# Re-timing the side work of a software-pipelined FNet and gated-convolution kernel

## The chip, the core and the metric

The kernel runs on one core of a Trainium2 chip. The metric is the device time of one execution in microseconds (us), as the median of repeated runs. The engines are named as in the profile: PE (TensorE matmuls), PEld (its weight loads), DVE (VectorE), ACT (ScalarE), POOL (GpSimd), SP (SyncE, which only issues transfers here).

## What is computed

```python
x: (8, 3136, 256) float32
X = np.fft.fft(np.fft.fft(x, axis=1), axis=2).real       # FNet mixing
h = np.maximum(X @ w_in, 0.0)                            # (8, 3136, 1024)
hp = h padded by one row of zeros at both ends of the sequence
conv_out = sum(conv_w[k] * hp[:, k:k + 3136] for k in range(3))
out = (h / (1 + np.exp(-conv_out))) @ w_out              # (8, 3136, 256)
```

All of it is float32. There are eight batches; the sequence transform of a batch has 3136 points.

## The kernel before

**Main pipeline.** The sequence is cut by symmetry into four chunks of output rows per batch (`CUTS`), and the 1024 hidden features into `NF` = 8 blocks of 128. A step is one (batch, chunk, feature block): 8 x 4 x 8 = 256 steps, 32 to a batch (`per`). The loop at the end of the kernel runs over cycles t, and one cycle holds stages of several steps. This is the order in which a cycle hands its instructions to the in-order queues of the engines:

- `sigmoid(t-2)` on ACT (L713)
- `products(t+1)`: the matmuls of `pb` and `pa` on PE, which finish the transforms and apply the input weights (tiles `qt`, `pt`, `G`); `copies(t+1)` on ACT brings `pb` to SBUF (L677)
- the side work "act"
- `combine(t)` on DVE: adds `pa` and the copy and clips at zero (two instructions, L688), which gives `h`
- the side work "load", then the side work "dve"
- `seed(t+2)` and `first_tap(t)` on ACT (L643, L694)
- `other_taps(t-1)` on DVE (two instructions, L700)
- `gate(t-2)`: one half of the product with the sigmoid on POOL (L720), the other on DVE (L721; L723 for a rest in the last chunk)
- `mm2(t-3)` on PE: twelve matmul instructions into `po`, fourteen in the last chunk of every second batch; after the eighth feature block ACT copies the result out and SP stores it
- the side work "pe"

PSUM has one buffer for `pb`, two for `pa`, four for `po` and one (`pd`) for the side work.

**Side work.** While the steps of batch b-1 run, batch b is prepared by operations that the table `side` spreads over the cycles, through `at(cycle, where, fn)`:

- *Loads* (`load_ops`): half a batch is one plain load and, for the second half, three one-row loads, all from SP, and four indirect loads (`mirrored`, L133), which POOL issues.
- *Folds* (`fold_ops`): 14 operations per batch on DVE, seven per half (`pair`, `both`, `evens`, `feats`; L158 to L187), which add and subtract mirrored rows and columns.
- *Sums of the DFT* (`units`): eight units per batch, each of four products on PE (`Unit.matmuls`, into `pd`), where needed a copy on ACT (`Unit.copy`, L287 and L306), and two sums on DVE (`Unit.fin`, L291/L294, L310/L312, L322/L324). Two units of a batch have no copy. A unit's copy and sums stand in the cycle after its last product, and in that cycle DVE runs the sums between `combine` and `other_taps`.
- *The column* (`Feature`): one column of the transform that needs a small DFT of its own. `place` loads tables, `gather` fetches 3136 single elements per batch into `ft`, `tables` and `stage` compute. It is done twice, for batches 1 to 3 and 4 to 7.

In the kernel before, the folds of batch b occupy the cycles from the end of the previous folds to `stop`, evenly spread, and the products of batch b run from `stop` to cycle 32b-3:

```python
    for b in range(1, B):
        stop = per * (b - 1) + max(28 - 8 * b, 2)
        fold_at[b] = (end, stop - end)
        dft_at[b] = (stop, per * b - 3 - stop)
        end = stop
```

So `stop` is 20, 44, 68, 98, 130, 162 and 194. Folds of batch b+1 and units of batch b lie over the same cycles, with no regard for each other. The loads of the next batch start in the cycle after the last fold of the half they replace, two indirect loads to a cycle. The gathers of the column go out from ACT, three in cycle 7 and four in cycle 20.

Of the kernel before, what the change touches and what calls it, by code (L numbers as in the profile page):

```python
# [31 lines left out]
RC = 56  # L32
# [6 lines left out]
def kernel(  # L39
# [10 lines left out]
    nc = tc.nc  # L50
    B, S, D = x.shape
    F = moe_w_in.shape[1]
    P = 128
# [9 lines left out]
    NF = F // P  # L63
# [27 lines left out]
    act = nc.scalar.activation  # L91
# [19 lines left out]
    def load_ops(b, h, eng, other=None, held=False):  # L111


        def plain():
            t = xp.tile([P, 8, 2, D], F32, name="xh", tag="xh")
            xh[b, h] = t
            if held:

                nc.gpsimd.memset(t[0:1, 0, 0, 0:1], 0.0)
            eng.dma_start(out=t[0:NP, 0:4], in_=bass.AP(  # L120
                tensor=x.tensor, offset=x.offset + (b * S + 1 + 2 * h) * D,
                ap=[[HQ * D, NP], [Q4 * D, 4], [1, 2 * D]]))

        def zero():
            t = xh[b, h]
            for s0, n, r in ((0, 4, 0), (4, 3, 1), (7, 1, 0)):
                (other or eng).dma_start(out=t[NP:KR, s0:s0 + n], in_=bass.AP(
                    tensor=x.tensor, offset=x.offset + (b * S + r * Q4) * D,
                    ap=[[D, 1], [Q4 * D, n], [0, 2], [1, D]]))

        def mirrored(m):
            def f():
                nc.gpsimd.indirect_dma_start(  # L133
                    out=xh[b, h][0:NP, 7 - m].rearrange("p q d -> p (q d)"),
                    out_offset=None,
                    in_=bass.AP(tensor=x.tensor, offset=x.offset,
                                ap=[[2 * D, B * S // 2], [1, 2 * D]]),
                    in_offset=bass.IndirectOffsetOnAxis(ap=idx[0:NP, 0:1], axis=0),
                    element_offset=(b * S + (4 - m) * Q4 - HO + 2 * (1 - h)) * D)
            return f  # L140
        return [plain] + [zero] * h + [mirrored(m) for m in range(4)]

    def fold_ops(b):

        def half(h):
            k = slice(0, NP if h == 0 else KR)
            qs = slice(2 * h, 2 * h + 2)  # L150

            def t():
                return xh[b, h]

            def pair(m):
                def f():
                    a, r = t()[k, m:m + 2], t()[k, 7 - m:5 - m:-1, ::-1, :]
                    vt(a[:, :, :, 1:D], a[:, :, :, 1:D], r[:, :, :, D - 1:0:-1], op=ALU.add)  # L158
                    if m == 2:
                        a, r = t()[k, 0:4], t()[k, 7:3:-1, ::-1, :]  # L160
                        vt(a[:, :, :, 0], a[:, :, :, 0], r[:, :, :, 0], op=ALU.add)
                return f

            def flat(i, j):
                return t()[k, i:j].rearrange("p s q d -> p (s q d)")

            def both(to, op):
                def f():
                    vt(flat(to, to + 2), flat(0, 2), flat(2, 4), op=op)  # L169
                return f  # L170

            def evens():
                vt(flat(0, 1), flat(4, 5), flat(5, 6), op=ALU.add)
                vt(flat(1, 2), flat(4, 5), flat(5, 6), op=ALU.subtract)  # L174

            def feats(odd):
                def f():
                    if h == 0 and odd:
                        wt[b] = [wp.tile([P, 4, HQ, P], F32, name="w", tag="w%d" % i) for i in range(2)]
                        if b == 0:  # L180
                            ea[b] = ep.tile([P, 2, HQ], F32, name="ea", tag="ea")
                            nc.gpsimd.memset(wt[b][0][0:KR, 2:4, :, P - 1:P], 0.0)
                    w, s = wt[b][odd], 6 * odd
                    v = t()[k, s:s + 2]
                    lo, hi = v[:, :, :, 1:P], v[:, :, :, D - 1:P:-1]
                    vt(w[k, 0:2, qs, 1:P], lo, hi, op=ALU.add)  # L186
                    vt(w[k, 2:4, qs, 0:P - 1], lo, hi, op=ALU.subtract)  # L187
                    nc.gpsimd.tensor_copy(w[k, 0:2, qs, 0], v[:, :, :, 0])  # L188
                    if b:
                        nc.gpsimd.memset(wt[b][odd][k, 2:4, qs, P - 1:P], 0.0)  # L190
                    elif odd:
                        gt(w[k, 2:4, qs, P - 1], t()[k, 7:5:-1, :, P], sg[k], op=ALU.mult)
                    else:
                        nc.gpsimd.tensor_copy(ea[b][k, :, qs], v[:, :, :, P])
                return f

            return [pair(0), pair(2), both(6, ALU.subtract), feats(1), both(4, ALU.add), evens,
                    feats(0)]

        return half(0) + half(1)  # L200
# [173 lines left out]
    class Feature:  # L374
# [39 lines left out]
                        tensor=dft_seq.tensor, offset=dft_seq.offset + (2 * r + s) * NQ * HE,  # L414
                        ap=[[4 * NQ * HE, n], [HE, NQ], [1, w]]))

        def gather(self, b0, b1):
            for b in range(b0, b1):
                nc.scalar.dma_start(out=self.y[self.K, b - b0].unsqueeze(2), in_=bass.AP(  # L419
                    tensor=x.tensor, offset=x.offset + b * S * D + P,  # L420
                    ap=[[RC * D, RC], [D, RC], [1, 1]]))

        def tables(self, i):
            H, K = self.H, self.K
# [40 lines left out]
    def spread(b, cs):  # L465

        for c in cs:
            ch = chunks[c]
            eb[b, c] = ebp.tile([P, HN], F32, name="eb", tag="eb")[:, 0:ch.k1 - ch.k0]
            nc.sync.dma_start(out=eb[b, c], in_=ed[b:b + 1, ch.k0:ch.k1].to_broadcast([P, ch.k1 - ch.k0]))  # L470
# [284 lines left out]
    begin, us, row, flip, store = units(0)  # L755
# [37 lines left out]
    per = len(chunks) * NF  # L793
    side = {}

    def at(cycle, where, fn):
        side.setdefault((cycle, where), []).append(fn)
# [9 lines left out]
        at(NF + 1 + j // 3, "load", fn)  # L807


    fold_at, dft_at = {}, {}  # L810
    end = 9
    for b in range(1, B):
        stop = per * (b - 1) + max(28 - 8 * b, 2)
        fold_at[b] = (end, stop - end)
        dft_at[b] = (stop, per * b - 3 - stop)
        end = stop
    for b in range(1, B):
        ops = fold_ops(b)
        c0, n = fold_at[b]
        cs = [c0 + j * n // len(ops) for j in range(len(ops))]  # L820
        assert b > 1 or cs[7] > NF + 3
        if b + 1 < B:
            for h in range(2):
                c1 = cs[7 * h + 6] + 1
                for j, fn in enumerate(load_ops(b + 1, h, nc.sync)):
                    at(c1 + (j + 1) // 2, "load", fn)
        for j, fn in enumerate(ops):
            at(cs[j], "dve", fn)
        begin, us, *_ = units(b)
        us = us[0:4] + us[5:]  # L830
        c0, n = dft_at[b]
        at(c0, "pe", begin)
        cs = [c0 + i * n // len(us) for i in range(len(us) + 1)]
        for i, u in enumerate(us):
            k = cs[i + 1] - cs[i]
            for j in range(k):
                at(cs[i] + j, "pe", lambda u=u, j=j, k=k: u.matmuls(j, k))
            at(cs[i + 1], "act", u.copy)
            at(cs[i + 1], "dve", u.fin)
        at(cs[-1] - 2, "load", lambda b=b: spread(b, range(len(chunks) - 1)))  # L840
        at(per * b + 1, "load", lambda b=b: spread(b, [len(chunks) - 1]))

    feat = Feature()
    at(5, "load", feat.place)
    for c, b0, b1 in ((7, 1, min(4, B)), (20, 4, B)):
        at(c, "load", lambda b0=b0, b1=b1: feat.gather(b0, b1))
    for i in range(3):
        at(11 + i, "act", lambda i=i: feat.tables(i))
    for c, b0, b1 in ((14, 1, min(4, B)), (per, 4, B)):
        for i, where in enumerate(("pe", "dve", "pe", "act")):  # L850
            at(c + i + (i > 2), where, lambda i=i, b0=b0, b1=b1: feat.stage(i, b0, b1))

# [1 line left out]
    n = len(steps)  # L856
# [4 lines left out]
    for t in range(n + LAG):  # L861
        def run(where):
            for fn in side.get((t, where), []):
                fn()
        if 0 <= t - 2 < n:
            sigmoid(steps[t - 2])
        if t + 1 < n:
            products(steps[t + 1])
            copies(steps[t + 1])
        run("act")  # L870
        if t < n:
            combine(steps[t])
        run("load")
        run("dve")
        if t + 2 < n:
            seed(steps[t + 2])
        if t < n:
            first_tap(steps[t])
        if 0 <= t - 1 < n:
            other_taps(steps[t - 1])  # L880
        if 0 <= t - 2 < n:
            gate(steps[t - 2])
        if t >= LAG:
            mm2(steps[t - LAG])
        run("pe")
# [66 lines left out]
```

## Time and profile before

| | |
|---|---|
| time, median of 3 runs | 1238.14 us (1236.81 to 1238.31) |
| profiled span | 1236.5 us |
| PE, DVE, ACT, POOL busy | 1189.9, 1136.0, 878.1, 378.4 us |
| matmuls of `mm2` (`po`) | 3072 instructions, 711.6 us |
| taps on DVE (L700) | 512 instructions, 555.5 us |
| chain that ended last | PE 71%, DVE 18%, issue 4%, ACT 3% |

In the timeline each line has the start, the busy time, the engine, the line of the kernel, the operation with its output and inputs, how many equal instructions were merged, and in brackets the engine's idle time before it with what ended it. A busy PE is a model of pipelined matmuls, so the length of a cycle is best read from the start of one `pb<-qt,G` group to the start of the next. In the table of windows each engine's column is its busy time in that stretch with the number of instructions.

### The profile page before, as it was taken

To read this page: it belongs to the slowest core of one execution; us is meant where nothing else is said; L and a number is where in the kernel's file an instruction comes from. 1 tells how busy PE (TensorE), PEld (TensorE's weight loads), DVE (VectorE), ACT (ScalarE), POOL (GpSimd) and SP (SyncE) were. 2 spreads that over 40 slices of the span, in tenths; PEclk is the share of its full clock that TensorE was granted. 3 is DMA by queue.
4 is the path that set the end of the run, shared out by engine and by line. 5 is a ranking of instruction groups with operands and counts; after the bars stand their busy time and mean duration, and the time that the engine had idled before them with its cause. 6 is when DMAs were issued, how large, how long until landed. Compare 5 with 4: busy or idle time off the path is not lost.

```text
span 1236.5 us, 15434 instructions
## 1 busy us (share of the span) xinstructions
PE 1189.9 (96%) x4876; PEld 908.4 (73%) x4876; DVE 1136.0 (92%) x1696; ACT 878.1 (71%) x1832; POOL 378.4 (31%) x474
## 2 busy tenths in 40 slices
PE   5998989899999999999999999999999999999998
PEld 4666667677777777677777777777777777777776
DVE  7799979999999989999999999999899888899996
ACT  2467646686677776777777777787777777788884
POOL 5225431433324241342324223242122211222222
PEclk9999999999999999999999999999999999999999
DMA  9504241211222120210212111120001000110000
GB/s 226 183 7 79 79 55 46 85 28 52 65 66 76 33 65 14 75 56 26 79 38 67 31 52 52 45 86 26 9 18 52 31 26 27 39 39 27 26 27 30
DMA packets 70213, 66.30 MB, mean 54 GB/s; under 512 B 28123, under 2 KB 57827, under 8 KB 70131
## 3 DMA queue, kind: packets, MB, share of 16 engines
q1 hardware_dynamic: 42443, 52.09, 13.7%
q0 software_dynamic: 5120, 12.85, 3.5%
q10 hardware_dynamic: 22568, 0.36, 1.3%
q8 instruction: 39, 0.64, 0.2%
q14 instruction: 43, 0.35, 0.1%
HBM read 39.53 MB, written 25.74 MB: 53 GB/s over the span
## 4 chain that ended last, share of the span: by engine, by line
PE 71%; DVE 18%; issue 4%; ACT 3%; DMA 1%; ACTq 0%; SPq 0%; DVEq 0%
PE po L94 43%; PE pb L94 10%; PE pa L94 10%; PE pd L94 7%; DVE g L700 6%; DVE g L721 2%; DVE h L688 2%; DVE xh L158 2%; ACT nb L677 1%; DVE w L187 1%; DVE xh L169 1%; DVE w L186 1%; DMA xh<-in_x_dram 1%; ACT g L713 1%; ACTq L419 0%
## 5 line engine op out<-in xcount | busy, mean ns | idle before, releaser
L94 PE MATMUL po<-wout,g 128*128 128x256 f32 x3072 | 711.6, 381 | 18.2 <-DVE g L721 18.2
L94 PEld LDWEIGHTS po<-wout,g 128*128 128x128 f32 x3072 | 580.8, 190 | 173.0 <-DVE g L721 50.0
L700 DVE SCALAR_TENSOR_TENSOR g<-h,cw,g 128x770 f32<-128x770 f32 (+1 forms) x512 | 555.5, 1085 | 9.8 <-ACT g L694 0.7
L720 POOL TENSOR_TENSOR g<-g,h 128x385 f32<-128x385 f32 (+1 forms) x256 | 241.0, 942 | 793.3 <-ACT g L713 536.3
L713 ACT ACTIVATE g<-g 128x385 f32<-128x385 f32 (+2 forms) x512 | 244.4, 527 | 200.7 <-DVE g L700 199.5
L677 ACT ACTIVATE nb<-pb 128x386 f32<-128x386 f32 (+2 forms) x472 | 208.2, 494 | 81.4 <-PE pb L94 80.5
L688 DVE CUSTOM_DVE_ANT_0 h<-pa,nb 128x386 f32<-128x386 f32 (+2 forms) x492 | 255.5, 559 | 3.7 <-ACT h L674 3.7
L694 ACT ACTIVATE g<-h,cw 128x770 f32<-128x770 f32 (+1 forms) x256 | 243.6, 951 | 0.2 <-DVE h L688 0.2
L94 PE MATMUL pa<-pt,G 128*128 128x387 f32 (+2 forms) x512 | 212.5, 496 | 7.5 <-ACT pa L643 7.5
L94 PE MATMUL pb<-qt,G 127*128 127x387 f32 (+2 forms) x512 | 212.6, 496 | 0.0
L643 ACT ACTIVATE pa<-eb,ge 128x387 f32<-128x387 f32 (+2 forms) x252 | 151.8, 603 | 15.8 <-issue 11.6
L94 PEld LDWEIGHTS pa<-pt,G 128*128 128x128 f32 x512 | 96.6, 189 | 82.1 <-issue 18.6
L721 DVE TENSOR_TENSOR g<-g,h 128x385 f32<-128x385 f32 (+1 forms) x256 | 145.4, 568 | 1.4 <-ACT g L713 1.4
L94 PE MATMUL pd<-tab,w 98*128 98x196 f32 (+3 forms) x448 | 120.9, 374 | 0.0
L94 PEld LDWEIGHTS pb<-qt,G 127*128 127x128 f32 x512 | 94.7, 190 | 17.4 <-issue 1.0
L133 POOL DMA_INDIRECT xh<-in_x_dram,idx x64 | 97.9, 1529 | 15.4 <-issue 13.0
L94 PEld LDWEIGHTS pd<-tab,w 98*128 98x128 f32 (+1 forms) x448 | 83.6, 190 | 12.7
L740 ACT COPY os<-po 128x256 f32<-128x256 f32 x196 | 58.2, 394 | 8.5 <-PE po L94 5.5
L158 DVE TENSOR_TENSOR xh<-xh 98x1020 f32<-98x1020 f32 (+1 forms) x32 | 46.7, 1465 | 3.8 <-DMA xh<-in_x_dram,idx 3.8
L169 DVE TENSOR_TENSOR xh<-xh 98x1024 f32<-98x1024 f32 (+1 forms) x32 | 40.6, 1269 | 0.1
L188 POOL COPY w<-xh 98x4 f32<-98x4 f32 (+1 forms) x32 | 27.4, 856 | 13.3 <-DVE xh L174 7.4
L291 DVE TENSOR_TENSOR qt<-as,pd 128x197 f32<-128x197 f32 (+1 forms) x14 | 7.2, 514 | 19.9 <-ACT as L287 19.9
(114 smaller groups left out, 392.8 us busy)
## 6 DMA issues: line engine op xcount, KB each, us to landing
out_dram<-os SPq DMA_DIRECT2D x192, 128.0 KB
xh<-in_x_dram SPq DMA_DIRECT2D x16, 784.0 KB
eb<-ed SPq DMA_DIRECT2D x16, 193.5 KB
tab<-dft_seq_dram SPq DMA_DIRECT2D x4, 589.5 KB
raw<-in_moe_w_in_dram SPq DMA_DIRECT2D x4, 512.0 KB
raw<-in_moe_w_out_dram SPq DMA_DIRECT2D x1, 2048.0 KB
eb<-ed SPq DMA_DIRECT2D x8, 209.0 KB
eb<-ed SPq DMA_DIRECT2D x8, 193.0 KB
```

The costliest lines, as they stand in the source:

```text
L94: nc.tensor.matmul(o, l, r, start=start, stop=stop, skip_group_check=True)
L133: nc.gpsimd.indirect_dma_start(out=xh[b, h][0:NP, 7 - m].rearrange("p q d -> p (q d)"), out_offset=None, in_=bass.AP(tensor=x.tensor, offs ...
L158: vt(a[:, :, :, 1:D], a[:, :, :, 1:D], r[:, :, :, D - 1:0:-1], op=ALU.add)
L643: act(pa[s][:, 0:n], eb[b, c], AF.Copy, scale=ge[:, f:f + 1])
L677: act(nb[s][:, i, cols], p[:, cols], AF.Copy, scale=-1.0 if i else 1.0)
L688: nc.vector._custom_dve(TENSOR_ADD_SAT, out=to, in0=a[:, cols], in1=c[:, i, cols], s0=BIG, s1=0.0)
L694: act(gs[s], hs[s][:, 0:n], AF.Copy, scale=cw[:, 0, s[2]:s[2] + 1])
L700: stt(out=g, in0=h[:, k:k + n], scalar=cw[:, k, f:f + 1], in1=g, op0=ALU.mult, op1=ALU.add)
L713: act(gs[s][:, c], gs[s][:, c], AF.Sigmoid)
L720: gt(g[:, p], g[:, p], h[:, p], op=ALU.mult)
L721: vt(g[:, v], g[:, v], h[:, v], op=ALU.mult)
L740: nc.scalar.copy(out=osb[:, j % 2], in_=pt[:, j % 2])
```

## The change

The change re-times the side work; it neither adds nor removes a computation.

- Folds get cycles of their own. The set `taken` collects the cycles that hold a unit's sums or the DVE stage of the column, and `free` moves a fold to the next cycle that is not taken, one fold to a cycle. This holds for batches 2 to 7; batch 1 keeps its cycles.
- The boundaries `ends` replace `stop`: 20, 46, 72, 98, 125, 157, 189. From batch 5 on the products of a batch take 32 cycles, one product to a cycle.
- The side work "load" is emitted after `gate`, where it stood before the side work "dve". Indirect loads go one to a cycle.
- The gathers of the column go out from SP, one to a cycle: cycles 6 to 8 and 21 to 24. The second run of the column's stages starts a cycle earlier (31).

```diff
-        def gather(self, b0, b1):
-            for b in range(b0, b1):
-                nc.scalar.dma_start(out=self.y[self.K, b - b0].unsqueeze(2), in_=bass.AP(
-                    tensor=x.tensor, offset=x.offset + b * S * D + P,
-                    ap=[[RC * D, RC], [D, RC], [1, 1]]))
+        def gather(self, b, b0):
+            nc.sync.dma_start(out=self.y[self.K, b - b0].unsqueeze(2), in_=bass.AP(
+                tensor=x.tensor, offset=x.offset + b * S * D + P, ap=[[RC * D, RC], [D, RC], [1, 1]]))
...
+    ends = [9] + [max(26 * b - 6, per * (b - 1) - 3) for b in range(1, B)]
+    taken = set()
+    def free(cycle):
+        while cycle in taken:
+            cycle += 1
+        taken.add(cycle)
+        return cycle
...
+    for c, b0, b1 in ((6, 1, min(4, B)), (21, 4, B)):
+        for b in range(b0, b1):
+            at(c + b - b0, "load", lambda b=b, b0=b0: feat.gather(b, b0))
-    for c, b0, b1 in ((14, 1, min(4, B)), (per, 4, B)):
+    for c, b0, b1 in ((14, 1, min(4, B)), (per - 1, 4, B)):
...
+        taken.add(c + 1)
...
             at(cs[i + 1], "dve", u.fin)
+            taken.add(cs[i + 1])
...
-        cs = [c0 + j * n // len(ops) for j in range(len(ops))]
+        cs = [free(c0 + j * n // len(ops)) if b > 1 else c0 + j * n // len(ops) for j in range(len(ops))]
...
-                c1 = cs[7 * h + 6] + 1
                 for j, fn in enumerate(load_ops(b + 1, h, nc.sync)):
-                    at(c1 + (j + 1) // 2, "load", fn)
+                    at(cs[7 * h + 6] + 1 + j, "load", fn)
...
             combine(steps[t])
-        run("load")
         run("dve")
...
             gate(steps[t - 2])
+        run("load")
         if t >= LAG:
             mm2(steps[t - LAG])
```

More of the change, by code (lines that the diff above doesn't have):

```diff
@@ L807 @@
         at(NF + 1 + j // 3, "load", fn)
-    fold_at, dft_at = {}, {}
-    end = 9
-    for b in range(1, B):
[L813 to L819, printed above, removed]
-        cs = [c0 + j * n // len(ops) for j in range(len(ops))]
-        assert b > 1 or cs[7] > NF + 3
-        if b + 1 < B:
-            for h in range(2):
-                c1 = cs[7 * h + 6] + 1
-                for j, fn in enumerate(load_ops(b + 1, h, nc.sync)):
-                    at(c1 + (j + 1) // 2, "load", fn)
-        for j, fn in enumerate(ops):
-            at(cs[j], "dve", fn)
+    ends = [9] + [max(26 * b - 6, per * (b - 1) - 3) for b in range(1, B)]
[5 more added lines that the diff above has]
+        return cycle
+    feat = Feature()
+    at(5, "load", feat.place)
+    for c, b0, b1 in ((6, 1, min(4, B)), (21, 4, B)):
+        for b in range(b0, b1):
+            at(c + b - b0, "load", lambda b=b, b0=b0: feat.gather(b, b0))
+    for i in range(3):
+        at(11 + i, "act", lambda i=i: feat.tables(i))
+    for c, b0, b1 in ((14, 1, min(4, B)), (per - 1, 4, B)):
+        for i, where in enumerate(("pe", "dve", "pe", "act")):
+            at(c + i + (i > 2), where, lambda i=i, b0=b0, b1=b1: feat.stage(i, b0, b1))
+        taken.add(c + 1)
+    for b in range(1, B):
         begin, us, *_ = units(b)
         us = us[0:4] + us[5:]
-        c0, n = dft_at[b]
-        at(c0, "pe", begin)
+        c0, n = ends[b], per * b - 3 - ends[b]
+        at(max(c0, per * (b - 1) + 1), "pe", begin)
         cs = [c0 + i * n // len(us) for i in range(len(us) + 1)]
@@ L839 @@
             at(cs[i + 1], "dve", u.fin)
+            taken.add(cs[i + 1])
         at(cs[-1] - 2, "load", lambda b=b: spread(b, range(len(chunks) - 1)))
         at(per * b + 1, "load", lambda b=b: spread(b, [len(chunks) - 1]))
[L843 to L848, printed above, removed]
-    for c, b0, b1 in ((14, 1, min(4, B)), (per, 4, B)):
-        for i, where in enumerate(("pe", "dve", "pe", "act")):
-            at(c + i + (i > 2), where, lambda i=i, b0=b0, b1=b1: feat.stage(i, b0, b1))
+    for b in range(1, B):
+        ops = fold_ops(b)
+        c0, n = ends[b - 1], ends[b] - ends[b - 1]
+        cs = [free(c0 + j * n // len(ops)) if b > 1 else c0 + j * n // len(ops) for j in range(len(ops))]
+        assert cs[-1] < ends[b] and (b > 1 or cs[7] > NF + 3)
+        if b + 1 < B:
+            for h in range(2):
+                for j, fn in enumerate(load_ops(b + 1, h, nc.sync)):
+                    at(cs[7 * h + 6] + 1 + j, "load", fn)
+        for j, fn in enumerate(ops):
+            at(cs[j], "dve", fn)
     LAG = 3
```

## The prediction

> **What bounds the kernel now.** I read the table of windows first, because a share of busy time over the whole span mixes stages. I cut it at starts of the `pb<-qt,G` matmuls, that is at cycles of the loop: rows 1 to 4 below are cycles 66-97, 98-129, 130-161 and 162-193 (32 each), row 5 is cycles 194-221 (the sums of batch 7, no folds), row 6 is 24 cycles near the end with no side work at all.
>
> ```profile
> core 0: us, PE busy (x) PEld busy (x) DVE busy (x) ACT busy (x) POOL busy (x), PEclk, DMA share, GB/s
> 384.54:529.90 145.36, 141.66 (x580) 107.97 (x579) 137.36 (x209) 107.25 (x223) 49.25 (x58) 1.00 0.19 58
> 529.90:675.21 145.31, 143.42 (x591) 110.62 (x590) 136.61 (x210) 108.43 (x224) 47.59 (x57) 1.00 0.16 51
> 675.21:818.99 143.78, 140.90 (x580) 108.35 (x579) 135.82 (x205) 106.96 (x222) 46.38 (x56) 1.00 0.16 51
> 818.99:964.30 145.31, 143.41 (x592) 110.61 (x591) 136.01 (x210) 108.45 (x224) 38.45 (x51) 1.00 0.10 32
> 964.30:1088.11 123.81, 123.81 (x516) 96.66 (x515) 104.21 (x158) 94.27 (x198) 25.32 (x33) 1.00 0.10 33
> 1092.28:1185.75 93.47, 93.47 (x386) 72.82 (x385) 92.62 (x129) 78.73 (x164) 23.27 (x33) 1.00 0.08 26
> ```
>
> Rows 5 and 6 have no gap on PE: there PE is the bound. Row 6 gives a bare cycle: 93.47 / 24 = 3.895 us. The timeline adds: 0.105 for a last-chunk `products`, 0.43 where `mm2` has fourteen matmuls, about 0.34 for a product of 196 columns and 0.66 for one of 392. Row 5 checks it: 123.81 less 28 x 3.895, 8 x 0.105 and 0.43 leaves 13.5 us for a batch's 32 products. So PE alone would need 124.64 + 0.84 + 13.5 = 139.0 us for a batch, plus 0.43 for each long `mm2` (1, 7, 1, 7 in rows 1 to 4): 139.5, 142.1, 139.5, 142.1. Measured less this floor: 5.8, 3.2, 4.2, 3.2. The same sum gives 3.1 for cycles 46-65 and 7.9 for cycles 22-45. That is 27.4 us in which PE waits, and folds are present in all of it.
>
> Then the table of waits, for who ends them:
>
> ```profile
> PEld po L94 <- DVE g L721: 50.0, 68, 2.9
> ```
>
> `mm2` waits for DVE's half of the gate. The timeline of cycle 143, where a fold (L186, L187) shares the cycle with a unit's sums (L291, L294), shows how:
>
> ```profile
> 735.29 0.52 DVE L291 TENSOR_TENSOR qt<-as,pd 128x196 f32<-128x196 f32 x1 [1.06 <-ACT as L287]
> 735.65 0.52 DVE L294 TENSOR_TENSOR qt<-pd,as 128x196 f32<-128x196 f32 x1
> 736.00 0.68 DVE L186 TENSOR_TENSOR w<-xh 98x508 f32<-98x508 f32 x1
> 736.60 0.67 DVE L187 TENSOR_TENSOR w<-xh 98x508 f32<-98x508 f32 x1
> 737.20 2.07 DVE L700 SCALAR_TENSOR_TENSOR g<-h,cw,g 128x770 f32<-128x770 f32 x2
> 739.18 0.56 DVE L721 TENSOR_TENSOR g<-g,h 128x385 f32<-128x385 f32 x1
> 739.65 0.56 DVE L688 CUSTOM_DVE_ANT_0 h<-pa,nb 128x386 f32<-128x386 f32 x1
> ```
>
> ```profile
> 739.79 0.48 PE L94 MATMUL po<-wout,g 128*128 128x256 f32 x1 [0.78 <-DVE g L721]
> ```
>
> The sums wait for ACT's copy, which uses up whatever DVE was ahead; then the fold delays taps and gate by 737.20 - 736.00 = 1.20 us, and PE waits. The cycle takes 5.27 instead of 4.23.
>
> Last, the gathers in cycle 20, in ACT's timeline and in PE's, and the clock after them:
>
> ```profile
> 160.10 4.58 ACTq L419 DMA_DIRECT2D ft<-in_x_dram  x2
> 164.74 0.59 ACT L643 ACTIVATE pa<-eb,ge 128x387 f32<-128x387 f32 x1 [6.78 <-issue]
> ```
>
> ```profile
> 165.38 1.36 PE L94 MATMUL pa<-pt,G 128*128 128x387 f32 x2 [3.78 <-ACT pa L643]
> ```
>
> ```profile
> 165.72:169.12 3.40, 3.40 (x9) 2.37 (x8) 1.12 (x3) 3.40 (x8) 1.94 (x3) 0.50 0.46 3
> ```
>
> ACT is held by issuing, so its `seed` is late, PE stands 3.78 us, and its clock is then halved for 3.4 us. Cycle 21 takes 12.27 us against a floor of 6.54: 5.7 lost.
>
> [...] here gaps of 3.78 and 2.28 us sufficed while one of 2.83 us at 92.86 did not. [...] a POOL gate behind two indirect loads at 744.03 meets the taps, which take 2.77 instead of 2.07 us.
>
> **The change part by part.**
>
> *Folds.* I keep an account of DVE's slack, from trace numbers alone. DVE's own cycle is 3.39 us (from L700 at 737.20 to the next at 740.59), 0.35 more in the last chunk. So a cycle gains slack of its floor less 3.39: 0.5 bare, 0.85 with a short product, 1.2 with a long one. A fold costs 1.2; sums cost 0.55, 0.7 or 1.0 by kind; the column's DVE stage costs 1.1. Sums that wait for a copy set the slack to about 0.1 in a cycle of 4.23 (in cycle 143 the fold cost 1.20 and PE lost 1.04), to more in longer ones. Slack holds at most 4 us: `gate(t-3)` may run almost two cycles late. What goes below zero PE waits.
>
> Run over the old order it gives, for cycles 22-45, 46-65 and the four rows above: 4.7, 3.7, 5.8, 3.4, 4.6, 3.4, against 7.9, 3.1, 5.8, 3.2, 4.2, 3.2 read. It falls short only in 22-45, where PE's clock was halved once (1.7) and the column's stages stand. Run over the new order: 8.6, 1.9, 3.9, 2.1, 3.3, 1.7. For instance before, cycle 143 lost 1.1 and cycle 157 (sums and `evens` together) 1.7; after, the sums of 141 leave 0.08, the folds of 142 and 143 cost 0.35 each beyond the 0.85 regained, and 0.24 and 0.47 are lost. From cycle 46 on that is 20.9 before and 12.9 after in the account; scaled to the 19.5 read, 12.0 remain: **7.5 us won**.
>
> Cycles 22-45 go the other way. Before, folds stood free of charge beside sums in cycles 23, 25, 26, where four products make PE's floor 5.3 to 6.5 us. Now `taken` pushes them past 29, and cycles 30, 31, 33 to 40 hold a fold each and 32 the column's stage, with bare PE cycles of 3.9. Each loses 1.2 - 0.5 = 0.7: 8.6 in all, against 7.9 read before with its halved clock. **0.7 lost.** No gap there exceeds 1.3 us, so I expect no halving.
>
> *Gathers.* ACT's seven issues, 0.85 to 2.9 us each, go to SP. What is queued behind them on SP: in cycles 6 to 8 the plain load of cycle 9, which waits for `w_out` to be narrowed in cycle 7 anyway; in 21 to 24 three one-row loads and, from cycle 26, stores. The first users are the matmuls of cycles 14 and 31. The first group waits on PE for matmuls that have long run, the second for the column's earlier stages. Nobody on the path waits for SP then. So the 5.7 of cycle 21 come back whole. In cycle 8 (7.65 us, its like take 4.54) only about half of 3.1 does: DVE narrows weights until 93.02, its gate starts at 95.01, and `mm2` waits for that instead. **7.2 won.**
>
> *Loads behind the gate, one a cycle.* POOL idles most of the time; nothing waits for L720 in the table of waits. What goes is the collision above: the 60 taps in such cycles took 3.4 us over the normal, nearly all within the slack. **0.3 won**, 0 to 2. The later loads have five cycles or more before their fold, against 3.9 us to land (transfer list). In the instruction order `place` now has DVE wait for POOL behind its gate in cycle 5, up to 1 us; but `seed` no longer stands behind its four issues on ACT (2.85 us of wait before). I take zero for both.
>
> Sum: 7.5 - 0.7 + 7.2 + 0.3 = 14.3; 1238.1 - 14.3 = 1223.8, rounded to **1224 us**.
>
> **Rivals.**
>
> *Folds give little.* DVE is busy 136 us of 144 a batch either way. If folds back to back after sums lose what was won, or a fold after sums costs 1 us rather than 0.3, the fold part shrinks to zero: 1238 - 7 = 1231. For it: pairs 126/127, 142/143, 158/159 stand together. Against: the account fits the old order to 0.6 us per stretch.
>
> *More is won.* Staggered loads also remove collisions on the slack, and cycle 8 comes back whole: 4 us more, 1220, or 1216 with the folds' loss halved again. For: L700 ranges to 2.77. Against: these slow taps are few.
>
> *Slower.* The packed folds of cycles 28 to 44 cost 1.3 each because DVE meets POOL's gate (up to 0.5 a cycle), [...] and SP's issues delay stores or the `eb` rows for batch 1: 15 lost against 13 won, about 1240. Against: SP mostly waits for ACT's copies (850 us of waits).
>
> **How the numbers follow.** Forecast (1219 to 1228) 0.60; little from folds (1228 to 1234) 0.22; more won (1214 to 1219) 0.09; no change 0.04; slower 0.05. Faster is the sum of the first three, 0.91. The range for 8 in 10 is 1217 to 1232.
>
> **What would show it.** Right: in the windows of cycles 98-193 about 1.5 us less per 32; no cycle over 10 us in the first 250 us, and PEclk at 1.00 there; no wait of ACT L643 on issue; seven gathers on SP's queue. Wrong: PE waits for L721 after cycle 98 as often as before, or a new wait for SP's transfers (`eb`, `xh`) on ACT or DVE.

## The result and the profile after

The changed kernel takes 1223.7 us (median of 4 runs, 1223.19 to 1223.94) against 1238.2 for the kernel before, timed beside it. The ratio is 0.9885, with a 95% interval of 0.9867 to 0.9902. The profiled span is 1222.2 instead of 1236.5 us.

I cut the trace again at the starts of the `pb<-qt,G` matmuls, which in the changed kernel fall at 375.44, 520.46 and so on for the same cycles 66, 98, 130, 162 and 194. This is the table of windows of the kernel after, with the columns as before:

```profile
core 0: us, PE busy (x) PEld busy (x) DVE busy (x) ACT busy (x) POOL busy (x), PEclk, DMA share, GB/s
375.44:520.46 145.02, 142.03 (x579) 108.11 (x578) 138.00 (x211) 107.25 (x223) 44.10 (x58) 1.00 0.18 57
520.46:666.66 146.20, 145.66 (x601) 112.28 (x600) 138.26 (x214) 107.97 (x224) 53.21 (x60) 1.00 0.17 55
666.66:808.54 141.88, 140.96 (x579) 108.52 (x578) 133.99 (x206) 107.46 (x223) 45.20 (x56) 1.00 0.17 52
808.54:951.92 143.38, 143.07 (x591) 110.97 (x590) 131.98 (x206) 108.23 (x223) 30.28 (x48) 1.00 0.09 28
```

The second row is longer than before (146.20 against 145.31), and that is no loss: it now holds batch 5's first products (601 matmuls instead of 591), which stood in the third row. PE's idle part, sum less busy, shows the gain: 1.9, 2.9 and 1.9 us in rows 2 to 4 before, 0.5, 0.9 and 0.3 now. In the first row it stays: 3.7 before, 3.0 now.

Here are cycles 141 to 143 of the kernel after, DVE's timeline:

```profile
716.91 0.52 DVE L291 TENSOR_TENSOR qt<-as,pd 128x196 f32<-128x196 f32 x1 [1.58 <-ACT as L287]
717.27 0.52 DVE L294 TENSOR_TENSOR qt<-pd,as 128x196 f32<-128x196 f32 x1
717.62 2.04 DVE L698 SCALAR_TENSOR_TENSOR g<-h,cw,g 128x770 f32<-128x770 f32 x2
719.58 0.56 DVE L719 TENSOR_TENSOR g<-g,h 128x385 f32<-128x385 f32 x1
720.05 1.02 DVE L686 CUSTOM_DVE_ANT_0 h<-pa,nb 128x386 f32<-128x386 f32 x2
720.99 1.27 DVE L158 TENSOR_TENSOR xh<-xh 99x1020 f32<-99x1020 f32 x1
722.18 2.06 DVE L698 SCALAR_TENSOR_TENSOR g<-h,cw,g 128x770 f32<-128x770 f32 x2
724.16 0.55 DVE L719 TENSOR_TENSOR g<-g,h 128x385 f32<-128x385 f32 x1
```

The sums still wait for ACT's copy (1.58), but the taps follow them at once. The fold (L158) comes a cycle later, when some slack has been regained. PE feels a fold one cycle after DVE runs it, because `mm2` takes the gate of the cycle before: the 5.27 us that the prediction gives for cycle 143 are, counted at the `pb<-qt,G` starts, those of cycle 144 (cycle 143 itself took 4.23). In the changed kernel cycle 142, after the sums, takes 4.23 us, its floor. Cycle 143, after the first fold, takes 4.41, and cycle 144, after the second, 4.71: 0.17 and 0.48 over their floors. Before, the one fold behind the sums cost 1.04.

The gathers of batches 4 to 7 in SP's timeline, and ACT's copy and seed in cycle 21, both after:

```profile
151.98 0.91 SPq L418 DMA_DIRECT2D ft<-in_x_dram  x1
152.93 5.65 SPq L127 DMA_DIRECT2D xh<-in_x_dram  x3
158.69 4.92 SPq L418 DMA_DIRECT2D ft<-in_x_dram  x3
```

```profile
159.67 0.32 ACT L306 COPY as<-pd 128x196 f32<-128x196 f32 x1
159.87 0.61 ACT L641 ACTIVATE pa<-eb,ge 128x387 f32<-128x387 f32 x1
```

SP is busy issuing from 151.98 to 163.61 and nobody waits for it; the seed follows the copy without a gap. SP waits for nobody either, so the gathers of cycles 22 to 24 leave back to back, all before cycle 22 begins on PE (164.50): "one to a cycle" is the order in the program, not in time. Cycle 21 takes 6.53 us instead of 12.27.

In the chain that ended last, DVE has a larger share than before (18%) and PE a smaller one (71%). It is one chain of many, and I rest nothing on it:

```profile
PE 68%; DVE 22%; issue 4%; ACT 2%; DMA 0%; DVEq 0%; SPq 0%; ACTq 0%
```

### The profile page after: what moved, and what is told of

Read it like the earlier page. It is cut to its first block, busy times and chain, and to the rows that moved or that the text cites. A ratio compares the mean times of both kernels' runs of the same rounds, so it can differ in the third digit from the quotient of the medians.

```text
span 1222.2 us, 15450 instructions
## 1 busy us (share of the span) xinstructions
PE 1187.9 (97%) x4876; PEld 907.5 (74%) x4876; DVE 1126.0 (92%) x1696; ACT 877.0 (72%) x1832; POOL 370.9 (30%) x474
## 4 chain that ended last, share of the span: by engine, by line
PE 68%; DVE 22%; issue 4%; ACT 2%; DMA 0%; DVEq 0%; SPq 0%; ACTq 0%
PE po L94 42%; PE pb L94 10%; PE pa L94 10%; DVE g L698 7%; PE pd L94 7%; DVE h L686 4%; DVE g L719 3%; DVE xh L158 2%; DVE xh L169 1%; ACT nb L675 1%; DVE w L186 1%; DVE w L187 1%; DVE xh L173 0%; ACT g L711 0%; DVE pt L291 0%
## 5 line engine op out<-in xcount | busy, mean ns | idle before, releaser
L94 PE MATMUL po<-wout,g 128*128 128x256 f32 x3072 | 709.9, 381 | 13.8 <-DVE g L719 13.3
L698 DVE SCALAR_TENSOR_TENSOR g<-h,cw,g 128x770 f32<-128x770 f32 (+1 forms) x512 | 548.9, 1072 | 9.3 <-ACT g L692 0.2
L718 POOL TENSOR_TENSOR g<-g,h 128x385 f32<-128x385 f32 (+1 forms) x256 | 232.5, 909 | 781.3 <-ACT g L711 523.1
L133 POOL DMA_INDIRECT xh<-in_x_dram,idx x64 | 106.5, 1665 | 13.4 <-issue 9.6
L94 PEld LDWEIGHTS pd<-tab,w 98*128 98x128 f32 (+1 forms) x448 | 84.0, 191 | 12.5
L158 DVE TENSOR_TENSOR xh<-xh 98x1020 f32<-98x1020 f32 (+1 forms) x32 | 40.8, 1283 | 2.4 <-DMA xh<-in_x_dram,idx 2.4
L291 DVE TENSOR_TENSOR pt<-as,pd 128x197 f32<-128x197 f32 (+1 forms) x14 | 7.3, 520 | 20.2 <-ACT as L287 20.2
```

Source lines behind the costliest of these rows:

```text
L94: nc.tensor.matmul(o, l, r, start=start, stop=stop, skip_group_check=True)
L133: nc.gpsimd.indirect_dma_start(out=xh[b, h][0:NP, 7 - m].rearrange("p q d -> p (q d)"), out_offset=None, in_=bass.AP(tensor=x.tensor, offs ...
L698: stt(out=g, in0=h[:, k:k + n], scalar=cw[:, k, f:f + 1], in1=g, op0=ALU.mult, op1=ALU.add)
L718: gt(g[:, p], g[:, p], h[:, p], op=ALU.mult)
```

## The experiments

Each kernel was traced and timed beside the kernel before. To compare them, I took the length of every cycle from the timeline and subtracted the floor of the prediction. The sum over a stretch is the time that PE lost there, in us:

| kernel | time, us | ratio to before (95%) | cycles 0-21 | 22-45 | 46-193 |
|---|---|---|---|---|---|
| before | 1238.0 to 1238.6 | | 22.1 | 7.9 | 19.5 |
| after | 1223.7 | 0.9885 (0.9867-0.9902) | 13.8 | 9.1 | 12.5 |
| e1 gathers only | 1231.4 | 0.9945 (0.9929-0.9962) | 16.2 | 7.2 | 19.6 |
| e2 loads only | 1231.8 | 0.9947 (0.9930-0.9964) | 18.6 | 6.7 | 19.0 |
| e3 folds only | 1233.3 | 0.9958 (0.9944-0.9972) | 23.3 | 10.1 | 13.5 |
| e4 gathers from ACT | 1223.4 | 0.9881 (0.9864-0.9897) | 13.9 | 9.1 | 12.2 |
| e5 before, folds ahead | 1227.6 | 0.9904 (0.9887-0.9920) | 24.6 | 7.9 | 7.0 |
| e6 e5 with e1 and e2 | 1214.1 | 0.9802 (0.9786-0.9818) | 14.4 | 6.0 | 5.8 |
| e7 batch 2 shares | 1219.7 | 0.9849 (0.9832-0.9865) | 13.9 | 5.8 | 12.2 |
| e8 loads ahead | 1223.7 | 0.9881 (0.9864-0.9897) | 15.0 | 9.1 | 12.2 |
| e9 after, folds ahead | 1211.4 | 0.9781 (0.9767-0.9794) | 14.4 | 3.9 | 5.6 |
| e10 e9, other `ends` | 1210.9 | 0.9770 (0.9757-0.9783) | 15.2 | 3.9 | 4.2 |

The start of the loop, which no edit touches, moves by up to 2 us from trace to trace (42.5 to 44.6 us). So the stretches tell more than the totals. A constant in the floor of a stretch falls out when two kernels are compared; only such differences are used below.

**e1: the gathers alone.** The kernel before with the changed `gather`:

```diff
-        at(c, "load", lambda b0=b0, b1=b1: feat.gather(b0, b1))
+        for b in range(b0, b1):
+            at(c + b - b0, "load", lambda b=b, b0=b0: feat.gather(b, b0))
```

> The kernel before, with only the gathers changed (from SP, one a cycle, cycles 6-8 and 21-24). Theory (ACT held by issuing costs PE the wait, and the halved clock after it): cycle 21 falls from 12.3 to 6.5-7 us, cycle 8 from 7.65 to about 6.3, PEclk 1.00 until cycle 33, everything after cycle 22 as before; 8 us less, about 1230. Rival (the gathers only move their cost, to SP's stores and eb rows, and the fold schedule carries the gain): 2 us less or nothing.

Cycle 21 fell to 6.53 and cycle 8 to 6.27, and cycles 46-193 did not move: the theory holds. But 5.9 us were won in cycles 0-21, less than expected. Cycles 8 to 13 take 31.42 us against 31.57 before: what cycle 8 won (1.38), cycles 10 to 13 gave back. PE's wait in cycle 8, before and in e1:

```profile
95.70 0.92 PE L94 MATMUL pa<-pt,G 128*128 128x387 f32 x2 [2.83 <-ACT pa L643]
```

```profile
94.69 1.56 PE L94 MATMUL po<-wout,g 128*128 128x256 f32 x6 [1.45 <-DVE g L719]
```

With ACT's hold gone, PE waits for DVE's gate instead, here and again in cycles 11 and 13 (0.48 and 1.14; before, nothing and 0.91). DVE was late there anyway, and ACT's hold had only moved the wait forward.

**e2: the loads alone.** The kernel before, with

```diff
-                    at(c1 + (j + 1) // 2, "load", fn)
+                    at(cs[7 * h + 6] + 1 + j, "load", fn)
...
-        run("load")
         run("dve")
...
             gate(steps[t - 2])
+        run("load")
```

> The kernel before, with only the loads changed (behind the gate, indirect loads one a cycle). Theory: the slow taps beside POOL's late gate go, but lie within DVE's slack; 0 to 1.5 us less, about 1237.5. Rival (collisions of POOL and DVE are what makes PE wait for L721): 5 us less or more, in all batches.

It won 6 us, as much as the rival said, but not where the rival said: 46-193 moved by 0.5. (1.2 of the 6 are the loop's earlier start in this trace, 43.39 instead of 44.55.) The edit carries more than loads. `place` and the gathers are side work "load" too, and before they stood on ACT ahead of `seed` and `first_tap`; now they stand behind. Cycle 6 fell from 5.65 to 4.68 and cycle 21 from 12.27 to 10.71. Cycle 8 fell from 7.65 to 6.28, but as in e1 the cycles up to 13 gave it back (31.28 us for cycles 8 to 13). Cycle 16 fell from 6.72 to 6.06. The largest part is cycle 34 (9.86 to 7.16): PE's stall there is 1.26 us instead of 2.28, and the clock is not halved. In e1, which has the stall of 2.28 with a whole clock, the cycle takes 8.17, so about 1.7 of the 2.7 is the clock.

**e3: the folds alone.** The changed kernel with e1's and e2's edits undone; against the kernel before only this differs, besides the boundaries `ends`, the column's second run, and the order of registration, in which the column's stages now come ahead of the folds:

```diff
-        cs = [c0 + j * n // len(ops) for j in range(len(ops))]
+        cs = [free(c0 + j * n // len(ops)) if b > 1 else c0 + j * n // len(ops) for j in range(len(ops))]
```

> The changed kernel, with gathers (three and four at once from ACT, cycles 7 and 20) and loads (ahead of the side work on DVE, two a cycle) as before, so that only the schedule of folds, units and of the column's second run is changed. Theory: PE's waits in cycles 46-193 fall from 19.5 to about 12.5 us, cycles 22-45 stay at 8 to 9, cycle 21 at about 12; 5 to 6.5 us less, about 1232. Rival (the folds' own cycles matter little without the loads behind the gate): 2 us less or nothing.

46-193 fell by 6.0, 22-45 rose by 2.1: as the theory has it, a little less. Here cycle 21 took 14.39 and cycle 8 took 9.25. In cycle 8 the stall was as long as before (2.75 and 2.83), but the clock was halved behind it. In cycle 21 ACT was held longer by the same four gathers (7.73 us instead of 6.78), PE stood 4.73 us instead of 3.78, and the clock was halved for 6.83 us instead of 3.41. The second half of that, from 165.72 on, with PEclk in third place from the end:

```profile
165.72:169.12 3.40, 3.40 (x10) 2.68 (x9) 3.15 (x6) 2.06 (x5) 2.32 (x2) 0.50 0.21 71
```

**e4: engine or bunching?** The changed kernel, with

```diff
-            nc.sync.dma_start(out=self.y[self.K, b - b0].unsqueeze(2), in_=bass.AP(
+            nc.scalar.dma_start(out=self.y[self.K, b - b0].unsqueeze(2), in_=bass.AP(
```

> The changed kernel, with the gathers issued from ACT, still one a cycle. Theory (the harm was seven issues in two bunches; ACT has 1 to 2 us to spare in the wide cycles 21-24): an issue of about 1.9 us costs PE 0 to 0.7 in its cycle; 1223.7 to 1226.5. Rival (it is the engine: any issue on ACT holds seed and copies): 1229 or more.

No loss at all. ACT's timeline in cycles 21 and 22:

```profile
158.26 0.85 ACTq L418 DMA_DIRECT2D ft<-in_x_dram  x1
158.38 0.32 ACT L306 COPY as<-pd 128x196 f32<-128x196 f32 x1
...
164.24 0.83 ACTq L418 DMA_DIRECT2D ft<-in_x_dram  x1
```

One a cycle, the gathers of cycles 21 to 24 are issued in 0.82 to 0.85 us each. Four at once took 0.85, 2.90 and 4.58 for the last two. So ACT as such was not the harm, and the move to SP is not needed. Nor is the spreading, once they are on SP: in e1 the four go out back to back, from 156.27 to 165.44, and cycle 21 still takes 6.53. The harm needed both, a bunch and a queue on which `seed` stands behind it; either remedy alone removes it.

**e5: position instead of own cycles.** The kernel before, old cycles for everything; only, folds are handed to DVE ahead of the sums of their cycle.

```diff
-            at(cs[j], "dve", fn)
+            at(cs[j], "fold", fn)
...
+        run("fold")
         run("dve")
```

> The kernel before with its own cycles for everything; only, where a fold shares a cycle with a unit's sums, the fold is handed to DVE ahead of them. Theory (the harm of sharing is that the fold stands behind sums that wait for ACT, with all slack gone; ahead of them it fills DVE's wait): the account gives 6.3 us of PE waits in cycles 46-193 where 19.5 were read, cycles 22-45 unchanged; 13 us less, about 1225. Rival (what counts is DVE's work per cycle, wherever it stands): no change, 1238.

46-193 fell from 19.5 to 7.0 us, where the account gave 6.3 and the changed kernel has 12.5. The total fell 2 us less than expected, because cycle 21 took 14.61 instead of 12.27: the gathers held ACT longer (5.32 us for the last two), PE stood 4.86 us, and the clock was halved for 6.83 us. This is DVE's cycle 143 in e6, which has the same schedule of folds:

```profile
715.19 0.77 DVE L186 TENSOR_TENSOR w<-xh 98x508 f32<-98x508 f32 x1
715.88 0.67 DVE L187 TENSOR_TENSOR w<-xh 98x508 f32<-98x508 f32 x1
716.48 0.52 DVE L291 TENSOR_TENSOR qt<-as,pd 128x196 f32<-128x196 f32 x1
716.82 0.54 DVE L294 TENSOR_TENSOR qt<-pd,as 128x196 f32<-128x196 f32 x1
717.18 2.07 DVE L698 SCALAR_TENSOR_TENSOR g<-h,cw,g 128x770 f32<-128x770 f32 x2
```

The fold stands where DVE waited for ACT. The sums follow with no wait left, and the fold costs nothing: cycle 144, in which PE felt it before (5.27), takes 4.23.

**e6: the three together.** e5 with e1 and e2.

> The kernel before with folds ahead of the sums, the gathers from SP one a cycle and the loads behind the gate one a cycle, folds and units in their old cycles. Theory: cycles 0-21 as in the changed kernel (13.8 us of waits), 22-45 about 5.5, 46-193 about 6.5; 9 to 10 us below the changed kernel, about 1214. Rival (work per cycle counts): 1229 to 1231, above the changed kernel.

1214.1, as expected. In the table of windows, cycles 98-129 and 162-193 have no gap on PE left:

```profile
513.23:655.60 142.37, 142.37 (x591) 111.02 (x590) 136.01 (x211) 108.69 (x224) 48.23 (x57) 1.00 0.17 51
797.89:940.27 142.38, 142.38 (x592) 111.00 (x591) 136.06 (x211) 108.73 (x224) 41.69 (x53) 1.00 0.11 34
```

DVE is busy 136 us there, as before, so its work per cycle was never the bound in these batches.

**e7: where batch 2's folds went.** The changed kernel with `taken` left open in batch 1's cycles:

```diff
-            taken.add(cs[i + 1])
+            if b > 1:
+                taken.add(cs[i + 1])
```

> The changed kernel, but the folds of batch 2 may share cycles with the sums of batch 1 (cycles 21 to 29, whose floor on PE is 4.7 to 6.5 us). Theory (cycles 30-41 lose because these folds were pushed out of cycles in which they were free): waits in cycles 22-45 fall from 9.1 to about 6 us, the rest as in the changed kernel; 3 us less, about 1220.5. Rival (cycles 30-41 lose for another reason, the earlier second run of the column or the loads in 37-40): no change.

22-45 fell from 9.1 to 5.8, the rest is unchanged. Cycles 36 to 41 lose 0.8 in all instead of 4.4, while cycles 28 and 30 lose 1.4 more and cycle 31 loses 1.0 less. So pushing these folds out of the wide cycles is what costs, in 36 to 41 above all.

**e8: loads ahead, one a cycle.** The changed kernel, with

```diff
+        run("load")
         run("dve")
...
             gate(steps[t - 2])
-        run("load")
```

> The changed kernel, with the side work for loads ahead of DVE's side work again, still one indirect load a cycle and gathers from SP. Theory (the part of the load edit that pays is that place's four issues on ACT no longer stand ahead of seed): cycle 6 goes from 4.68 back to 5.65 us, cycle 16 stays at 5.9, otherwise within 0.5 us; 1224 to 1225.5. Rival (POOL's late gate collides with the taps once more): 2 to 4 us more, spread over the batches.

Cycle 6 is back at 5.66, cycles 0-21 lose 1.2 more, and 46-193 are as in the changed kernel. The time is the same (the loop started 1.4 us earlier in this trace). So in the changed schedule the place behind the gate pays only through `place`.

**e9 and e10: both versions in one.** The changed kernel with e5's edit and without the units' cycles in `taken`; e10 also moves the boundaries:

```diff
-            taken.add(cs[i + 1])
...
-    ends = [9] + [max(26 * b - 6, per * (b - 1) - 3) for b in range(1, B)]
+    ends = [9, 20, 46, 70, 94, 126, 158, 190]
```

> The changed kernel with the folds ahead of the sums and free to share their cycles (only the cycles of the column's DVE stage stay taken); units, gathers and loads as in the changed kernel. Theory (own cycles are second best to standing ahead of the wait): waits in cycles 22-45 about 4.5 us instead of 9.1, in 46-193 about 6.6 instead of 12.5; 10 us less than the changed kernel, about 1213.5. Rival (own cycles already give what can be had, and two operations in a cycle overfill it): 1223 or more.

> As the kernel with folds ahead in the changed schedule, with the boundaries ends at 20, 46, 70, 94, 126, 158, 190, chosen by the account of slack so that fewer folds fall into bare cycles at the end of a batch. Theory: 2 us of waits less in cycles 66-193, about 1211.5. Rival (the account is too coarse to choose by): within 1 us of it, either way.

e9 takes 1211.4 us, 12 below the changed kernel. In 0-21 it loses 0.6 more than the changed kernel, in cycles 16, 17 and 19. e10's boundaries win 1.4 us in 46-193, where the account had 2, but its clock was halved once in cycle 8 of this trace (0.998 in the mean), and the intervals of the two overlap: no difference is shown. The times differ by 0.5 us, as e10's rival had it.

## Why the prediction was right, step by step

The time was 1223.7 where 1224 was forecast. The parts of the change and the place of each gain are as forecast, but the sum is better than some of its terms. Changes of PE's loss by stretch, from the table: 8.3 won in cycles 0-21, 1.2 lost in 22-45, 7.0 won in 46-193, 0.3 at the loop's start. That makes 14.4 where 14.3 was forecast, from terms that were off by up to 1.3, some high and some low: that they cancelled is luck.

- **The floor and the account of slack hold.** The account gave 12.9 us for 46-193 (12.0 scaled); 12.5 were read. Stretch by stretch: 1.9, 3.9, 2.1, 3.3, 1.7 forecast from cycle 46 on, 1.4, 5.5, 2.1, 2.3, 1.3 read. The miss is cycles 66-97, where cycles 94, 95 and 97 alone lose 2.8. The fold term was 7.5, measured 7.0. The example of batch 6 came out: 0.24 and 0.47 forecast for the folds of cycles 142 and 143, 0.17 and 0.48 read. e5 shows the account's central assumption: the loss comes from standing behind sums that wait for a copy. A slip in the floor's working does no harm: row 5 holds seven last-chunk `products`, not eight, which makes 13.6 and 139.1, and from these the printed 139.5 and 142.1 follow.
- **Cycles 22-45 cost more, as said:** 0.7 forecast, 1.2 read. Cycles 36 to 41 lose 0.67 to 0.78 each, the 0.7 that was forecast for a fold in a bare cycle, and e7 shows the cause. The net is small because the largest stall of the old order went, where the column's stage shared a cycle with a fold: cycles 33 and 34 took 14.10 us together (cycle 34 in part at half clock) and take 10.35 now, as they do in e3. PE's clock stayed whole (PEclk 1.00).
- **The gathers were oversized in one place.** Cycle 21 gave its 5.7. Cycle 8 gave 1.4 as forecast, but the prediction stopped there; cycles 10 to 13 took it back. In e1 the two bunches together won 5.9, not 7.2. "From SP" was credited alone, though spreading them over cycles on ACT does as much (e4).
- **The load edit was undersized.** The prediction put 0.3 on POOL's collisions and zero on `place`. `place` behind the seed won 0.97 in cycle 6 (e8 gives it back). In the later batches the collisions of POOL and DVE were worth little, as said: from e8 to the changed kernel 46-193 do not improve (12.2 and 12.5). Another 1.2 us came in cycles 16 to 19, which the prediction did not have, and there a fold beside POOL's gate did count: 2.45 us instead of 1.20. This is the fold of cycle 15, before and after:

```profile
130.58 2.45 DVE L158 TENSOR_TENSOR xh<-xh 99x1020 f32<-99x1020 f32 x1
```

```profile
129.83 1.20 DVE L158 TENSOR_TENSOR xh<-xh 99x1020 f32<-99x1020 f32 x1
```

Before, POOL's gate ran beside it (131.06 to 131.94). In the new order of registration the column's DVE stage stands ahead of this fold, and the gate is over (129.71) when the fold starts. As far as these cycles go, e9 undoes just that order: the fold takes 1.78, and cycles 16 and 17 take 6.05 and 4.90 instead of 5.91 and 4.65. The load edit alone (e2) also brings 1.78 and 6.06.
- **The signs to watch.** PEclk was 1.00 in cycles 0 to 33, and ACT's seed no longer waits on issue. The waits of PE for the gate say two things. These are the lines for cycles 98-193, before and after, with the wait in us in total, how often, and the longest:

```profile
PEld po L94 <- DVE g L721: 18.7, 25, 2.0
PE po L94 <- DVE g L721: 6.7, 12, 1.3
```

```profile
PEld po L94 <- DVE g L719: 15.0, 30, 1.1
PE po L94 <- DVE g L719: 1.5, 6, 0.4
```

  The weight loads of `po` waited more often than before, though for less time; by their number, which is how the prediction had put it, the forecast would look wrong. The matmuls themselves waited half as often and for 1.5 us instead of 6.7.

The rival "folds give little" is refuted by e3, "slower" by the result. "More is won" failed because cycle 8's gain was given back and the staggered loads won nothing in 46-193, though e9 shows that more was to be had by another edit.

## What to carry to other kernels

Where an engine works through its instructions in order, look for the one that waits inside a cycle, and try side work ahead of it before giving it a cycle of its own. Here a fold of 1.2 us behind the wait cost 1.04, ahead of it nothing. That holds as far as the wait reaches: in cycle 15, where DVE had no wait and POOL's gate was running, the fold did better behind the column's stage (1.20 us after, 1.78 in e9). Take slow issues off a queue on which urgent work stands behind them, or spread them over cycles; here either was enough (cycle 21 took 6.53 us in e1 instead of 12.27, and cycles 0-21 lost 13.9 us in e4 against 13.8 after). And before crediting a stall with its length, see whether the next engine was late at the same place; then removing the stall only moves the wait.

## What the runs showed of the hardware

- **Issuing.** A gather of 3136 single elements was issued in 0.82 to 0.91 us when it did not follow another one, and in 1.9 to 2.9 us right behind another, on ACT (2.10 to 2.90 before) and on SP (1.92 to 2.30 after) alike. On SP three one-row loads behind a gather took 5.65 us after, instead of 2.12 before.
- **The clock.** Of stalls of like length, some were followed by PE's halved clock and some were not: 2.28 us in cycle 34 was in the kernel before (9.86 us) and was not in e1 (8.17); 2.83 us in cycle 8 was not in the kernel before, 2.75 in e3 was. The length of the stall alone does not tell them apart, and I draw no limit from these traces. This is cycle 34 of the kernel before, the 3.41 us that hold the stall (PE busy for 1.13) and the 3.41 us at half clock behind them:

```profile
233.98:237.39 3.41, 1.13 (x5) 0.49 (x4) 3.37 (x6) 0.89 (x3) 0.28 (x1) 1.00 0.00 0
237.39:240.80 3.41, 3.41 (x10) 2.70 (x9) 3.37 (x6) 3.02 (x9) 0.62 (x2) 0.50 0.05 17
```

  In cycle 21 the stall varied as well as the clock: 3.78 us and 3.41 us at half clock before (12.27 us), 4.73 and 4.86 us and 6.83 us at half clock in e3 and e5 (14.39 and 14.61).
